# A setup re-planned: second-stage angles on VectorE, four token weight products ahead of the mirrored weights, chunk 0's y evicted sooner

## The chip, the cores and the metric

The kernel runs on one core of one Trainium2 chip. The metric is the device time of one execution in microseconds (us); smaller is better. A time is quoted as the median of several executions with the lowest and highest in brackets. The profile is of one execution, and its span is some 2 us shorter than the time.

Engine names: PE is TensorE, DVE is VectorE, ACT is ScalarE, POOL is GpSimd, SP issues transfers.

## The reference, cut to what matters

```python
def _attn_ref(x):
    X = np.fft.fft(x, axis=1)          # over 3008 tokens
    X = np.fft.fft(X, axis=2)          # over 256 features
    return X.real.astype(np.float32)

def _moe_ref(x, w_tok1, w_tok2, w_ch1, w_ch2):
    xt = x.transpose(0, 2, 1)
    h = np.maximum(xt @ w_tok1, 0.0) @ w_tok2
    u = x + h.transpose(0, 2, 1)
    h2 = np.maximum(u @ w_ch1, 0.0) @ w_ch2
    return (u + h2).astype(np.float32)
# x: 8 x 3008 x 256; w_tok1: 3008 x 256; w_ch1: 256 x 1536
```

The output is the second function of the first. The Fourier transforms are done as matrix products with tables of sines and cosines, which the kernel builds on the chip while the first inputs and weights arrive. That is the setup.

## The kernel before

```python
# Angles of the second-stage table td, made on ACT and reduced on DVE.
for o, n, d, k, off in (...four stretches of md...):
    act(md[:, o:o + n], jrow[:, 0:n], scale=d[:, k:k + 1], ...)
whole(vd[:], md[:])                     # ACT
rest(md[:], vd[:], md[:])               # DVE
...
sin(td[:, 0:65], md[:, 0:65])           # ACT

# POOL: the small table anti, then all weight loads are issued by POOL.
ts(acol[:], pcol[:], -1.0, AT.mult, 127.0, AT.add, eng=G)
ts(anti[:], jrow[:, 0:P], acol[:], AT.is_equal, eng=G)
def load_rest():
    load_wc1(0)                         # wc: channel weights, first half
    ...w2n...
    load_wc1(1)                         # second half
    gdma(wc2[...], ...)                 # second channel weights
# later on POOL, when wc2 has landed: five sums over wc (t1w ... t4w)

# The order of the setup's work.
fold0 = fold(0, V)                      # DVE folds batch 0's input in two halves
filler(12)                              # PE: products whose result nobody reads
take(fold0, 5)                          # first half
ts(ol[:, 0:1], ol[:, 0:1], 2.0, AT.mult)                             # four small
ts(td[:, 0:1], td[:, 64:65], 0.5, AT.mult, ol[:, 0:1], AT.add)       # repairs of
ts(td[:, 65:66], td[:, 64:65], 0.5, AT.mult, ol[:, 0:1], AT.subtract)# td, on DVE
V.memset(td[:, 64:65], 0.0)
take(fold0, 5)                          # second half
own = front(0)                          # stage 1 of batch 0: products pz, results z
take(tu_q, 3); take(tu_p, 2)            # tables tq, tts on PE
take(own, 2)                            # stage 1, first half of the fold
take(tu_r, 3)
filler(4)
take(own, 2)                            # stage 1, second half of the fold
take(tu_b0, 2)
take(own, 4)
...
```

After stage 1 come the second-stage products (pw, from td and z), the token products (ph, from the tables tts and the weights w1p and w1m), and from there chunk after chunk of channel products (pc). Batch 1's input is xp, loaded in rows, and xm, gathered by index. Its fold on DVE (fa, fb, ..., pad) runs in the first chunks of batch 0.

Of the kernel before, what the change touches and what calls it, by code (L numbers as in the profile page):

```python
# [12 lines left out]
AT = mybir.AluOpType  # L13
AFT = mybir.ActivationFunctionType

P = 128
# [3 lines left out]
DTOK = 256  # L20
# [5 lines left out]
NG = 12  # L26
# [10 lines left out]
def kernel(  # L37
# [25 lines left out]
    def ps_mm(name):  # L63
        return psum.tile([P, 512], FP32, tag="mm", name=name, bufs=3)
# [4 lines left out]
    def ps_f(name, dt=FP32, n=512):  # L69
        return psum.tile([P, n], dt, tag="f", name=name, bufs=3)  # L70
# [11 lines left out]
    def ts(out_, in_, s1, op0, s2=None, op1=None, eng=V):  # L82
        if op1 is None:
            eng.tensor_scalar(out=out_, in0=in_, scalar1=s1, scalar2=None, op0=op0)
        else:
            eng.tensor_scalar(out=out_, in0=in_, scalar1=s1, scalar2=s2,
                              op0=op0, op1=op1)
# [7 lines left out]
    def act(out_, in_, scale=1.0, func=AFT.Copy, bias=None):  # L95
        kw = {} if bias is None else {"bias": bias}
        nc.scalar.activation(out=out_, in_=in_, func=func, scale=scale, **kw)  # L97

    def copy(e, out_, in_):
        if e:  # L100
            V.tensor_copy(out=out_, in_=in_)
        else:
            act(out_, in_)
# [111 lines left out]
    def whole(v, m):  # L215
        act(v, m, func=AFT.Identity, bias=tw23[0:m.shape[0], :])

    def rest(r, v, m):
        stt(r, v, -TWO23, m, AT.add, AT.subtract)
# [47 lines left out]
    ts(dr[:], q2[:], 1.0 / 128, AT.mult, 0.0, AT.max)  # L267
    stt(ol[:, 1:2], dl[:, 1:2], 0.5, ol[:, 1:2])
    ts(orr[:], dr[:], 0.5, AT.mult)
    for o, n, d, k, off in ((0, 65, dl, 0, ol[:, 0:1]), (65, 64, dr, 0, None),  # L270
                            (129, 64, dl, 1, ol[:, 1:2]), (193, 64, dr, 1, orr[:, 1:2])):
        if off is None:
            act(md[:, o:o + n], jrow[:, 0:n], scale=d[:, k:k + 1])
        else:
            act(md[:, o:o + n], jrow[:, 0:n], scale=d[:, k:k + 1], func=AFT.Identity, bias=off)
    whole(vd[:], md[:])

    ident, anti, lrot = (const.tile([P, P], FP16, tag=n, name=n)
                         for n in ("ident", "anti", "lrot"))
# [12 lines left out]
    t1b = const.tile([KR, 3, 24], FP16, tag="t1b")  # L292
    t1m = stage.tile([KR, 96], FP16, tag="t1m")
    t1c = stage.tile([KR, 72], FP16, tag="t1c")
    rest(md[:], vd[:], md[:])
    csv = cs[0:KR, 0:4, :].rearrange("p (a b) k -> p a b k", a=2)
    for i in range(2):
# [7 lines left out]
    sin(td[:, 66:258], md[:, 65:257])  # L305


    ts(acol[:], pcol[:], -1.0, AT.mult, 127.0, AT.add, eng=G)
    ts(anti[:], jrow[:, 0:P], acol[:], AT.is_equal, eng=G)
    wc1 = const.tile([P, 2, DCH], FP16, tag="wc1")  # L310
# [120 lines left out]
    def back(k, sgn):  # L431
        for c in range(3):
            c4 = slice(512 * c, 512 * c + 512)
            pr = ps_mm("pr")
            nc.tensor.matmul(pr[:], lhsT=anti[:], rhs=tts[k][:, c4], start=True, stop=True)
            if k:
                act(tts[k + 1][:, c4], pr[:], scale=sgn)
            else:
                V.tensor_copy(out=tts[k + 1][:, c4], in_=pr[:])
            yield  # L440

    hp = const.tile([P, NG, DTOK], FP16, tag="hp")
    hq = const.tile([P, NG, DTOK], FP16, tag="hq")

    def carried():
        for dst, t0, t1 in ((hp, tts[0], tts[1]), (hq, tts[2], tts[3])):
            for g2 in range(NG // 2):
                ph = ps_mm("ph")
                for k in range(2):
                    g = 2 * g2 + k  # L450
                    o = ph[:, k * DTOK:(k + 1) * DTOK]
                    nc.tensor.matmul(o, lhsT=t0[:, g * P:g * P + P], rhs=w1p[:, g, :],
                                     start=True, stop=False)
                    nc.tensor.matmul(o, lhsT=t1[:, g * P:g * P + P],
                                     rhs=w1m[:, NG - 1 - g, :],
                                     start=False, stop=True)
                copy(g2 % 2, dst[:, 2 * g2:2 * g2 + 2, :].rearrange("p g k -> p (g k)"),
                     ph[:])
                yield

# [2 lines left out]
    def front(b):  # L463
# [15 lines left out]
        for t0 in (11, 6, 1):  # L479
            for half in range(2):  # L480
                pz = ps_f("pz")
                for k in range(5):
                    stage1(pz[:, 96 * k:96 * k + 96], eo[:, t0 + k], half, t1r, t1m[:])
                zo = z[:, half, :, :].rearrange("p k (u s) -> p u k s", u=4)
                copy(half == 0 and b > 0, zo[:, :, :, t0:t0 + 5],
                     pz[:, 0:480].rearrange("p (t u k) -> p u k t", t=5, u=4))
                yield
        for half in range(2):
# [44 lines left out]
        def y(c):  # L533
            ps = []
            for o, tab in ((0, tp), (129, tq)):
                py = ps_f("py")
                for k in range(4):
                    nc.tensor.matmul(py[:, P * k:P * k + P], lhsT=w[:, 4 * c + k, o:o + P],  # L538
                                     rhs=tab[:, 4 * c + k, :], start=True, stop=True)
                ps.append(py)  # L540
                if o == 0:
                    yield
            sq = perb.tile([P, CW], FP32, tag="sqy", name="sqy", bufs=2)
            act(sq[:], ps[1][:])
            yield
            pv = ps[0][:].rearrange("p (g i b) -> p g i b", g=4, i=2)
            sv = sq[:].rearrange("p (g i b) -> p g i b", g=4, i=2)
            tt(ytg[:, 0, c], pv, sv, AT.subtract)
            tt(ytg[:, 1, c], pv, sv, AT.add)
            nc.sync.dma_start(out=yrow[c:c + 1], in_=yt[0:1, 1::-1, 8 * c:8 * c + 8, :])  # L550
            yield
# [30 lines left out]
        def tok1():  # L582
            for th in range(2):
                c = slice(th * P, (th + 1) * P)
                pt = ps_f("pt1")
                uv = perb.tile([P, 2, P], FP32, tag="uv", name="uv", bufs=2)
                for o, n, w0, hw in ((0, 129, 0, hp), (129, 127, 130, hq)):
                    if b == 0 and o:
                        sp = perb.tile([P, 129], FP32, tag="sp", name="sp", bufs=1)
                        act(sp[:], pt[:, 0:129])  # L590
                        pt = ps_f("pt2")
                        tt(uv[:, 0, 0:1], sp[:, 0:1], sp[:, P:129], AT.subtract)
                        tt(uv[:, 1, 0:1], sp[:, 0:1], sp[:, P:129], AT.add)
                    for g in range(NG):
                        nc.tensor.matmul(pt[:, o:o + n], lhsT=hw[:, g, c],  # L595
                                         rhs=w[:, g, w0:w0 + n],
                                         start=(g == 0), stop=(g == NG - 1))
                if b == 0:
                    tt(uv[:, 0, 1:], sp[:, 1:P], pt[:, 129:256], AT.subtract)
                    ts(uu[:, th, 0, :], uv[:, 0, :], 0.0, AT.max)  # L600
                    tt(uv[:, 1, 1:], sp[:, 1:P], pt[:, 129:256], AT.add)
                    act(uu[:, th, 1, :], uv[:, 1, :], func=AFT.Relu)
                    yield
                    continue
                sq = perb.tile([P, P], FP32, tag="squ", name="squ", bufs=1)
                act(sq[:], pt[:, P:2 * P])
                tt(uv[:, 0, :], pt[:, 0:P], sq[:], AT.subtract)
                tt(uv[:, 1, :], pt[:, 0:P], sq[:], AT.add)
                ts(uu[:, th, :, :], uv[:], 0.0, AT.max)
                yield  # L610
                if th == 0 and b > 0:
                    yield from rot()

        if b == 0:
            yield from rot()
            yield from y(0)
            yield from tok1()
            y1 = y(1)
            next(y1)
            next(y1)  # L620
            yield
            yield from tok2(0)
            yield from y1
            yield from tok2(1)
            yield from y(2)
            yield from tok2(2)
            for c in (4, 3, 5):
                yield from tok2(c)
        else:
            yield from tok1()  # L630
            for c in range(3):
                yield from y(c)
            for c in (2, 1, 0, 3, 4, 5):
                yield from tok2(c)
# [170 lines left out]
    def take(g, n):  # L805
        for _ in range(n):
            next(g, None)
# [6 lines left out]
    fold0 = fold(0, V)  # L814
    filler(12)
    take(fold0, 5)
    ts(ol[:, 0:1], ol[:, 0:1], 2.0, AT.mult)
    ts(td[:, 0:1], td[:, 64:65], 0.5, AT.mult, ol[:, 0:1], AT.add)
    ts(td[:, 65:66], td[:, 64:65], 0.5, AT.mult, ol[:, 0:1], AT.subtract)
    V.memset(td[:, 64:65], 0.0)  # L820
    take(fold0, 5)
    own = front(0)
    take(tu_q, 3)
    take(tu_p, 2)
    take(own, 2)
    take(tu_r, 3)
    filler(4)
    take(own, 2)
    take(tu_b0, 2)
    take(own, 4)  # L830
# [118 lines left out]
```

## Time and profile before

The kernel before took 601.85 us (601.52 to 602.42, three runs).

| | before |
|---|---|
| span of the profiled execution | 599.8 us |
| PE busy | 582.5 us, 97% |
| first channel product on PE | 33.63 us |
| fold of batch 1 starts on DVE | 42.12 us |
| product on pad starts on PE | 62.34 us |

The prediction below shows the page and the chain of waits.

### The profile page before, as it was taken

The page shows a single profiled execution, that of the slowest core. Times are in us where ns is not written, and L with a number is a line of the kernel's source. Part 1 is how long each engine was busy: PE and PEld are TensorE (multiplying, and loading weights), DVE is VectorE, ACT ScalarE, POOL GpSimd, SP SyncE. Part 2 cuts the span into 40 slices and gives each one's busy share as a digit, 9 for nine tenths or more (in the row PEclk, how much of TensorE's full clock was granted, in tenths as well). Part 3 has the DMA queues.
Part 4 walks back from the last instruction along what each step waited for, and adds up shares of the span by engine and source line. Part 5 has one row for each costly group of instructions (what it writes and reads, how often), then busy time and mean ns, then how long its engine had stood idle before and what let it go on. Part 6 is the DMA issues. An engine that isn't in the chain of part 4 may idle for free.

```text
span 599.8 us, 15331 instructions
## 1 busy us (share of the span) xinstructions
PE 582.5 (97%) x6273; PEld 417.8 (70%) x6273; DVE 449.5 (75%) x924; ACT 390.2 (65%) x753; POOL 255.1 (43%) x396
## 2 busy tenths in 40 slices
PE   3899999999999999999999999999999999999997
PEld 3756676677767776667767777677766777666776
DVE  8769879685898668766898668856688757966663
ACT  8764665478647865477656867568665786556662
POOL 8550545937555554626348444565555000000000
PEclk9999999999999999999999999999999999999999
DMA  8992822277138913394335753376133422323533
GB/s 158 207 192 61 170 50 53 61 149 119 37 71 121 149 37 68 78 181 54 68 84 91 135 89 55 67 147 113 37 60 80 93 55 55 77 61 77 93 72 88
DMA packets 83414, 55.69 MB, mean 93 GB/s; under 512 B 53778, under 2 KB 80082, under 8 KB 82578
## 3 DMA queue, kind: packets, MB, share of 16 engines
q1 hardware_dynamic: 76816, 36.82, 31.9%
q0 software_dynamic: 6208, 17.63, 16.2%
q8 instruction: 49, 0.80, 0.6%
q10 hardware_dynamic: 320, 0.26, 0.2%
q14 instruction: 21, 0.17, 0.1%
HBM read 35.26 MB, written 24.64 MB: 100 GB/s over the span
## 4 chain that ended last, share of the span: by engine, by line
PE 82%; DVE 1%; issue 0%; DVEq 0%
PE pc L662 36%; PE pa L712 17%; PE pb L712 13%; PE pu L566 6%; PE po L775 4%; PE pt L595 3%; PE pz L471 1%; PE py L538 1%; PE pw L512 1%; PE pw L508 1%; DVE s L90 1%; DVE osb L90 0%; DVE ut L90 0%; PE pz L496 0%; DVE q L90 0%
## 5 line engine op out<-in xcount | busy, mean ns | idle before, releaser
L97 ACT ACTIVATE c<-pc 128x512 f16<-128x512 f32 (+1 forms) x553 | 314.4, 591 | 156.2 <-PE pc L662 138.7
L662 PE MATMUL pc<-ut,wc 128*128 128x512 f16 (+1 forms) x1152 | 316.5, 374 | 1.2 <-DVE ut L90 1.2
L712 PEld LDWEIGHTS <-s 128*128 128x128 f16 x1968 | 123.5, 98 | 37.5 <-DVE s L90 0.6
L662 PEld LDWEIGHTS <-wc 128*128 128x128 f16 x1152 | 97.0, 98 | 50.7 <-issue 3.0
L712 PEld LDWEIGHTS <-c 128*128 128x128 f16 x1476 | 93.0, 97 | 27.8
L90 DVE TENSOR_TENSOR q<-pa,uT 128x256 f32<-128x256 f32 x123 | 52.5, 427 | 47.6 <-PE pa L712 47.5
L90 DVE TENSOR_TENSOR s<-c 128x1536 f16<-128x1536 f16 x82 | 80.7, 984 | 4.7 <-ACT c L97 4.7
L908 POOL COPY hold<-s 128x1 f16<-128x1 f16 x29 | 5.4, 187 | 173.5 <-DVE s L90 173.5
L90 DVE TENSOR_TENSOR osb<-pb,q 128x256 f32<-128x256 f32 x123 | 52.0, 422 | 23.8 <-PE pb L712 20.3
L90 DVE TENSOR_TENSOR ut<-pu,yt 128x512 f16<-128x512 f32 (+1 forms) x96 | 63.3, 672 | 0.8 <-PE pu L566 0.4
L90 POOL TENSOR_TENSOR eo<-sab 96x512 f16<-96x512 f16 x48 | 52.7, 1114 | 1.6
L566 PE MATMUL pu<-w2r,uu 128*128 128x512 f16 (+1 forms) x168 | 50.0, 379 | 0.3 <-DVE ut L90 0.3
L90 POOL TENSOR_TENSOR sab<-fa,fb 96x256 f16<-96x256 f16 (+1 forms) x72 | 46.7, 673 | 0.0
L90 DVE TENSOR_TENSOR s<-s,c 128x1536 f16<-128x1536 f16 x41 | 40.4, 986 | 0.0
L97 ACT ACTIVATE w<-pw 128x257 f16<-128x257 f32 x90 | 34.8, 387 | 8.4 <-PE pw L512 5.5
L90 DVE TENSOR_TENSOR s<-c,s 128x1536 f16<-128x1536 f16 x41 | 39.0, 952 | 0.0
L775 PE MATMUL po<-wc,c 128*128 128x256 f16 x288 | 35.4, 273 | 0.0
L712 PE MATMUL pb<-wc,c 128*128 128x128 f16 x492 | 34.4, 219 | 0.0
L712 PE MATMUL pa<-wc,c 128*128 128x128 f16 x492 | 34.4, 219 | 0.0
L712 PE MATMUL pa<-t2w,s 128*128 128x128 f16 x492 | 34.2, 219 | 0.1
L712 PE MATMUL pb<-t1w,s 128*128 128x128 f16 x492 | 34.2, 219 | 0.0
L712 PE MATMUL pa<-t4w,c 128*128 128x128 f16 x492 | 34.2, 219 | 0.0
(187 smaller groups left out, 728.0 us busy)
## 6 DMA issues: line engine op xcount, KB each, us to landing
out_dram<-osb SPq DMA_DIRECT2D x83, 256.0 KB
xp<-in_x_dram POOLq DMA_DIRECT2D x14, 408.0 KB, 6.4
out_dram<-osb SPq DMA_DIRECT2D x11, 192.0 KB
uT<-ut SPq DMA_TRANSPOSE x96
w2n<-in_moe_w_tok_dram POOLq DMA_DIRECT2D x2, 752.0 KB, 9.8
w1p<-in_moe_w_tok_dram POOLq DMA_DIRECT2D x2, 384.0 KB, 8.2
wc<-in_moe_w_ch_dram POOLq DMA_DIRECT2D x1, 768.0 KB, 15.3
xp<-in_x_dram POOLq DMA_DIRECT2D x2, 272.0 KB, 5.7
```

Source lines behind the costliest of these rows:

```text
L90: eng.tensor_tensor(out=out_, in0=a, in1=b, op=op)
L97: nc.scalar.activation(out=out_, in_=in_, func=func, scale=scale, **kw)
L471: nc.tensor.matmul(out_, lhsT=rows[:, half * P:half * P + P], rhs=tab, start=True, stop=True)
L508: nc.tensor.matmul(pw[:, 0:256].rearrange("p (h d) -> p h d", h=2)[:, :, 0:65], lhsT=zg[:, 0, g], rhs=td[:, 0:130].rearrange("p (h d) -> p ...
L512: nc.tensor.matmul(pw[:, 64:322].rearrange("p (h d) -> p h d", h=2)[:, :, 0:64], lhsT=zg[:, 1, g], rhs=td[:, 130:258].rearrange("p (h d) - ...
L538: nc.tensor.matmul(py[:, P * k:P * k + P], lhsT=w[:, 4 * c + k, o:o + P], rhs=tab[:, 4 * c + k, :], start=True, stop=True)
L566: nc.tensor.matmul(pu[:, 0:64 * nk], lhsT=uu[:, th, h, :], rhs=w2[:, th, :, 8 * c:8 * c + nk], start=(th == 0), stop=(th == 1))
L595: nc.tensor.matmul(pt[:, o:o + n], lhsT=hw[:, g, c], rhs=w[:, g, w0:w0 + n], start=(g == 0), stop=(g == NG - 1))
L662: nc.tensor.matmul(pc[:, 0:n], lhsT=wc1[:, h, ct * P:(ct + 1) * P], rhs=ut[:, c, h, 0:n], start=(h == 0), stop=(h == 1))
L712: nc.tensor.matmul(dst[:, P * a:P * a + P], lhsT=left[:, k, a, :], rhs=right[:, k, :], start=(first and k + a == 0), stop=(k == NH - 1), s ...
L775: nc.tensor.matmul(po[:, o:o + D], lhsT=c1[:, ct, ks * P:ks * P + P], rhs=wc2[:, ct, 0:D], start=(ct == 0), stop=(ct == NCT - 1))
L908: G.tensor_copy(out=hold[:], in_=pbox[3][:, 0, 0, 0:1])
```

## The change

The intent is to get PE to its first dense stretch sooner. The angles leave ACT, so that its large sine tp can start earlier. The four repairs of td leave DVE for POOL, between the fold's two halves. Four products on w1p take the place of four fillers ahead of the second half of stage 1 (the change's title says eight; four stand there). Stage-1 results are evicted by two engines, and y of chunk 0 is interleaved differently. Besides, the table products tu_r move ahead of the first half of stage 1, and a few evictions of tts and hq change engines (left out of the cut below).

```diff
-    for o, n, d, k, off in (...):
-        ...act(md[:, o:o + n], jrow[:, 0:n], scale=d[:, k:k + 1], ...)
-    whole(vd[:], md[:])
 ...
+    for o, n, d, k, off in (...):
+        ...ts(md[:, o:o + n], jrow[:, 0:n], d[:, k:k + 1], AT.mult, ...)
+    ts(vd[:], md[:], TWO23, AT.add)
     rest(md[:], vd[:], md[:])
 ...
+    ts(ol[:, 0:1], ol[:, 0:1], 2.0, AT.mult, eng=G)
+    ts(td[:, 0:1], td[:, 64:65], 0.5, AT.mult, ol[:, 0:1], AT.add, eng=G)
+    ts(td[:, 65:66], td[:, 64:65], 0.5, AT.mult, ol[:, 0:1], AT.subtract, eng=G)
+    G.memset(td[:, 64:65], 0.0)
     ts(acol[:], pcol[:], -1.0, AT.mult, 127.0, AT.add, eng=G)
     ts(anti[:], jrow[:, 0:P], acol[:], AT.is_equal, eng=G)
 ...
     def carried():
+        early = [ps_out("ph", k) for k in range(2)]
+        for g in range(4):
+            one(early[g // 2], tts[0], w1p, g, g, g % 2 == 0)
+        yield
 ...  # the other products follow, w1p first and then w1m, pair by pair
-                copy(half == 0 and b > 0, zo[:, :, :, t0:t0 + 5],
+                copy(half == 0 if b else half and t0 < 11, zo[:, :, :, t0:t0 + 5],
 ...
-            yield from y(0)
-            yield from tok1()
+            y0, t1 = y(0), tok1()
+            for piece in (y0, y0, y0, t1, t1):
+                next(piece)
+                yield
 ...
     take(fold0, 5)
-    ts(ol[:, 0:1], ol[:, 0:1], 2.0, AT.mult)
-    ts(td[:, 0:1], td[:, 64:65], 0.5, AT.mult, ol[:, 0:1], AT.add)
-    ts(td[:, 65:66], td[:, 64:65], 0.5, AT.mult, ol[:, 0:1], AT.subtract)
-    V.memset(td[:, 64:65], 0.0)
     take(fold0, 5)
     own = front(0)
     take(tu_q, 3)
     take(tu_p, 2)
+    take(tu_r, 3)
     take(own, 2)
-    take(tu_r, 3)
-    filler(4)
+    take(car, 1)
     take(own, 2)
```

## The prediction

> **What bounds the kernel now.** I read the page's busy shares and its 40 slices first. TensorE (PE) is busy 582.5 of 599.8 us; all its visible slack is in the first slice, 15 us long. So a change of setup can be worth a few us at most, and 2% of the run is 12 us.
>
> ```profile
> span 599.8 us, 15331 instructions
> PE 582.5 (97%) x6273; PEld 417.8 (70%) x6273; DVE 449.5 (75%) x924; ACT 390.2 (65%) x753; POOL 255.1 (43%) x396
> PE   3899999999999999999999999999999999999997
> ```
>
> Second, the timeline of PE (start, duration, engine, line, operation, in square brackets the idle time before it and what ended it). PE starts at 8.06, waits 1.19 us for VectorE's folded input at 16.02 and 0.41 for ScalarE's z at 19.86; then it is nearly dense until the first channel product at 33.63.
>
> ```profile
> 8.06 1.46 PE L399 MATMUL filler<-lrot,ident 128*128 128x128 f16 x12 [8.06 <-DVE ident L84]
> 16.02 0.93 PE L476 MATMUL pz<-t1n,eo 96*128 96x96 f16 x11 [1.19 <-DVE eo L90]
> 19.86 0.23 PE L508 MATMUL pw<-td,z 128*128 128x130 f16 x1 [0.41 <-ACT z L97]
> 20.21 0.27 PE L454 MATMUL ph<-w1m,tts 128*128 128x256 f16 x1
> 33.63 1.46 PE L662 MATMUL pc<-ut,wc 128*128 128x512 f16 x6 [0.32 <-DVE ut L90]
> 53.14 0.38 PE L662 MATMUL pc<-ut,wc 128*128 128x512 f16 x1 [0.90 <-DVE ut L90]
> 62.34 0.20 PE L496 MATMUL pz<-t1n,pad 96*128 96x24 f16 x2 [0.26 <-DVE pad L90]
> ```
>
> Third, what comes after setup, because a gain there counts only if it survives. The timeline of VectorE (DVE) shows a wait of 2.67 us for the second batch's input (the gathered half xm) until 42.12. From there DVE runs without a gap to 64.1; its next large wait for PE is at 67.75. The two PE waits above, at 53.14 and 62.34, are for results of that gapless run: pad is the end of the second batch's fold.
>
> ```profile
> 42.12 0.77 DVE L90 TENSOR_TENSOR fa<-xp,xm 96x508 f16<-96x508 f16 x1 [2.67 <-DMA xm<-in_x_dram,ix]
> 42.81 1.76 DVE L90 TENSOR_TENSOR fb<-xm,xp 96x508 f16<-96x508 f16 x1
> 44.50 0.18 DVE L90 TENSOR_TENSOR sab<-xp,xm 96x8 f16<-96x8 f16 x1
> 61.91 0.48 DVE L90 TENSOR_TENSOR pad<-sab 96x65 f16<-96x65 f16 x4
> 67.75 0.82 DVE L90 TENSOR_TENSOR osb<-po,uT 128x256 f32<-128x256 f32 x3 [1.55 <-PE po L775]
> ```
>
> Fourth, why xm lands only then: the DMA view of 20 to 45 us. In its 40 slices the DMA engines are full until the landing; the load is the tail of one long saturated queue.
>
> ```profile
> DMA  9998999999999999999999999999799999999999
> q0 software_dynamic: 2625, 4.51, 98.9%
> q1 hardware_dynamic: 1644, 0.40, 17.9%
> ```
>
> Fifth, GpSimd (POOL) in the same time: its weight sums start when the last weights land and end at 42.57 + 1.72 = 44.29.
>
> ```profile
> 36.83 0.23 POOL L646 COPY wc<-wc 128x12 f16<-128x12 f16 x1 [5.92 <-DMA wc<-in_moe_w_ch_dram]
> 41.10 1.51 POOL L90 TENSOR_TENSOR t3w<-b,wc 128x768 f16<-128x768 f16 x1
> 42.57 1.72 POOL L90 TENSOR_TENSOR t4w<-wc,t2w 128x768 f16<-128x768 f16 x1
> ```
>
> **What the Trainium skill says.** The page "SBUF — State Buffer", section "Who interferes with whom", calls the shared port pair an exclusive lock between VectorE and GpSimd, and counts a tensor_tensor with two SBUF inputs among what contends with GpSimd's reads. The trace agrees: fb took 1.76 us at 42.81, ending at 44.57, just after POOL's t4w; the same operation takes 0.41 at 47.36, with POOL idle. "DMA: Bandwidth & Descriptors", section "Issuing engines are not separate DMA queues", says that all issuers use the same 16 engines. In this trace q0 (the loads) fell from 0.21 MB in the microsecond from 40 to 0.14 MB in the next, when q1's packets (transposes issued by SP) rose to 239. "TensorE: Matmul & The Clock Gate", Part 1, has PE slow down after idling; here the granted clock is 0.999 on average, and I give the four removed fillers no cost.
>
> **The change, part by part.** The order view of the two programs gives the moves; beyond the chunk products of batch 0 the sequence on every engine is unchanged.
>
> 1. Angles. ScalarE loses four md and one vd activations, which occupy it from 6.57 to 8.35: 1.8 us. Its large sine (tp) then waits for DVE's m, 6.60 + 0.95 = 7.55, and starts 0.8 us earlier. The first product on tp, at 10.08, comes at about 9.3. DVE gains five small operations. A 128x120 tensor_scalar took 0.28 and a 128x128 one 0.28; I allow 4 x 0.16 + 0.35 = 1.0 us for the five. In before, DVE sat idle 0.47 for vd, so the remainder md moves from 8.48 to about 9.0. The small tables follow, ending at 10.3 in place of 9.8; the fold started at 10.13 because xm landed then, so it starts some 0.2 us late.
>
> 2. The td repairs leave DVE: first-half fold to second-half fold was 12.82 to 13.45, of which 0.6 us goes. Second half: 13.45 + 0.2 - 0.6, so about 13.05, 0.4 us earlier; PE's wait for eo ends at about 15.6 in place of 16.02. POOL carries them instead. Its small operations stand about 0.2 to 0.3 apart, so four make 0.9 us, and the loads issued from 15.12 go out at about 16.0. The queue then still has the mirrored weights (w1m), which land at 9.83 + 9.8 = 19.6, so I cost this at zero.
>
> 3. Products ahead. The words say eight; the order view shows four w1p products placed before the second group of stage-1 products, in place of four fillers. At 0.11 us of start-to-start each they take 0.44 us out of the later stretch. They need w1p: two issues at 6.44 and about 7.15, 7.6 to 8.8 us to land, hence 14.8 to 15.9. That lies in the gap, but can give back up to 0.3 us.
>
> 4. z on two engines. ScalarE's z evictions ran 16.95 + 2.85 = 19.80, five in a row at about 0.55 us. Now two of the large ones go to DVE and one tts eviction comes over. With stage 1 0.2 to 0.4 us earlier and a net saving of one eviction, 0.5, pw starts at about 19.1 to 19.2 in place of 19.86: 0.7 us. Then w1m stands in the way: the first such product was at 20.21 and cannot start before 19.6, so at most 0.6 us passes there.
>
> 5. y of chunk 0 and the last hq. The sequence on PE is the same; DVE gives one hq eviction to ScalarE. PE's wait of 0.19 for hq at 29.98 goes.
>
> Sum at the first channel product: 0.55 (w1m floor) + 0.2 (part of the early products that ScalarE's evictions do not hide; it is busy nearly throughout from 20 to 25 us) + 0.19 = about 0.9 us, so 33.63 becomes about 32.7. I hold 0.4 to 1.4 for possible.
>
> What reaches the end: nothing of it, by the third reading. The xm gather lands when the saturated queue is through, whatever PE does. DVE's order is fixed, so its idle time before the fold grows, from 2.67 towards 3.6; the gapless run starts at 42.12 as before; PE waits at 53.14 for 1.8 in place of 0.9; and by 62.34 both kernels are at the same point. Everything after that is the same program. The sum on the path is 0.
>
> **The rivals.**
>
> A. The gain survives, some 0.9 us, giving 600.9. This needs the landing or DVE's run to move too. For it: if xm came half a us earlier, fa and fb might slip between POOL's operations and escape the 1.35 us that fb lost. Against it: bytes and order of the loads are unchanged and the queue was full throughout.
>
> B. A loss, of 0.2 to 0.6 us, giving 602.2. An earlier PE makes the first transposes on q1 earlier, at about 40.4 in place of 41.3. They then share the DMA engines with the end of the xm gather for 0.9 us longer, at about half: 0.45 us later. POOL's t4w then has the lock, and fa waits until 44.3 with fb behind it. Since fb ended at 44.57 anyway, only about 0.25 to 0.4 of this is new. For it: q0 did fall by a third in that microsecond. Against it: PE must really be early.
>
> C. The longer DVE list delays the front. DVE has 1.0 us more before the fold, and if a small operation costs twice my figure the second half of the fold starts late and PE's gain is gone. This hardly touches the time: DVE idles 2.67 us before 42.12 and PE has 0.9 of wait at 53.14, so under 0.9 us of lateness disappears. It would give 601.8.
>
> **Range and chances.** The central case is no change; A at perhaps one in four pulls by 0.2, B at one in four pushes by 0.1, so 601.7. The three runs of before lie between 601.52 and 602.42, half a us either way of the median; with A's end of 600.9 and B's of 602.3, a range of 600.8 to 602.5 should hold it 8 times in 10. Twelve us one way or the other has no mechanism here: 1% each.
>
> **What would show it right or wrong.** In the new profile: tp's sine at about 7.6; z evictions on both engines and pw at about 19.2; PE waiting for no hq; first channel product near 32.7; DVE's idle before the second batch's fold longer than 2.67 and the fold still at 42.1 plus or minus 0.5; the PE wait near 53 about 1.8; pad reached at about 62.3. If the fold starts a us earlier or later, or if fb takes 0.41 there, the prediction's step on the landing is wrong and A or B holds. If PE stalls for w1p before the second stage-1 group, step 3 is wrong. It would be wrong as a whole if the span fell with the fold unmoved, since PE would then be making up the time somewhere after 62 that I take as equal.

## More of the kernel before

POOL's timeline. The columns are start, duration, engine, line, operation with output and input, sizes and count; a bracket, where there is one, gives the idle time just before and what ended it.

```profile
13.03 0.34 POOL L86 TENSOR_SCALAR ixc<-cfeat 128x1 int32<-128x1 f32 x2
...
13.72 1.45 POOL L84 TENSOR_SCALAR anti<-jrow,acol 128x128 f16<-128x128 f32 x1
15.12 1.17 POOL L106 DMA_DIRECT2D wc<-in_moe_w_ch_dram  x2
...
29.81 0.94 POOL L109 DMA_INDIRECT xm<-in_x_dram,ix  x1 [2.60 <-DMA w2n<-in_moe_w_tok_dram]
```

The small index operations take 0.17 us each, and the first channel weights are issued at 15.12. The last gather of batch 1's xm is issued only at 29.81, after a wait that the profile puts down to the landing of w2n. One line of PE is needed for comparison, two products on anti:

```profile
17.17 0.60 PE L435 MATMUL pr<-tts,anti 128*128 128x512 f16 x2
```

The windows view gives, for each stretch of 2 us, the busy time of PE, weight loads, DVE, ACT and POOL, then the clock granted to PE, the DMA share and the GB/s.

```profile
16.00:18.00 2.00, 1.86 (x32) 1.50 (x33) 1.23 (x7) 1.18 (x3) 1.70 (x3) 1.00 1.12 211
18.00:20.00 2.00, 1.49 (x31) 1.08 (x29) 1.61 (x4) 1.80 (x4) 1.74 (x4) 1.00 1.18 205
20.00:22.00 2.00, 2.00 (x22) 1.58 (x22) 1.43 (x4) 1.65 (x5) 1.69 (x3) 1.00 1.14 208
```

The granted clock is 1.00, and the DMA engines move 205 GB/s or more all the time. The DMA view of 16 to 24 us sums up what that is in bytes:

```profile
DMA packets 766, 1.67 MB, mean 209 GB/s; under 512 B 96, under 2 KB 416, under 8 KB 764
```

## The result, and the profile after

The changed kernel took 604.45 us (603.68 to 605.53, six runs), the kernel before 601.8 in the same rounds. The ratio is 1.0039, with a 95% interval of 1.0019 to 1.0059. The change is a small loss, 2 to 3 us, and it lies above the predicted range.

The page of the profiled execution, which took 603.68 us:

```profile
span 601.3 us, 15324 instructions
PEclk9899999999999999999999999999999999999999
```

The row PEclk is the granted clock in tenths in 40 slices of 15 us. The second slice has an 8, where before has nines throughout. PE's timeline:

```profile
16.51 0.61 PE L452 MATMUL ph<-w1p,tts 128*128 128x256 f16 x4 [1.95 <-DMA w1p<-in_moe_w_tok_dram]
...
18.38 1.05 PE L439 MATMUL pr<-tts,anti 128*128 128x512 f16 x2
...
21.73 0.23 PE L521 MATMUL pw<-td,z 128*128 128x130 f16 x1 [0.26 <-ACT z L97]
...
35.87 1.46 PE L677 MATMUL pc<-ut,wc 128*128 128x512 f16 x6 [0.25 <-DMA wc<-in_moe_w_ch_dram]
...
63.72 0.22 PE L509 MATMUL pz<-t1n,pad 96*128 96x24 f16 x2 [0.26 <-DVE pad L90]
```

The early products wait 1.95 us for w1p. The same two products on anti that took 0.60 us in before take 1.05. The first product on td and z comes 1.87 us later than before (19.86), and the first channel product 2.24 us later (33.63). The windows of 16 to 22 us name the reason for the 1.05:

```profile
16.00:18.00 2.00, 1.49 (x20) 1.45 (x21) 0.69 (x6) 0.18 (x1) 1.77 (x5) 0.79 1.12 210
18.00:20.00 2.00, 2.00 (x20) 1.45 (x18) 1.35 (x2) 1.16 (x2) 1.70 (x4) 0.50 1.06 167
20.00:22.00 2.00, 1.70 (x27) 1.25 (x25) 1.09 (x3) 1.26 (x3) 2.00 (x4) 0.86 0.80 99
```

The granted clock is 0.50 through the whole of 18 to 20 us. In windows of 0.2 us it is 0.50 from about 17.2 to 20.6. In the same rows the DMA engines fall from 210 to 167 and 99 GB/s, where before moved 205 and more. POOL's timeline and the DMA view of 16 to 24 us say why:

```profile
13.53 1.24 POOL L86 TENSOR_SCALAR ixc<-cfeat 128x1 int32<-128x1 f32 x2
...
15.06 1.27 POOL L86 TENSOR_SCALAR td<-td,ol 128x1 f16<-128x1 f16 x2
...
17.43 1.17 POOL L106 DMA_DIRECT2D wc<-in_moe_w_ch_dram  x2
...
30.98 0.93 POOL L109 DMA_INDIRECT xm<-in_x_dram,ix  x1 [2.75 <-DMA w2n<-in_moe_w_tok_dram]
...
43.57 1.73 POOL L90 TENSOR_TENSOR t4w<-wc,t2w 128x768 f16<-128x768 f16 x1
```

```profile
DMA packets 726, 1.38 MB, mean 173 GB/s; under 512 B 97, under 2 KB 417, under 8 KB 725
```

Two operations of 128 x 1 elements take 1.27 us, and the two index operations grew from 0.34 to 1.24. The loads are issued 2.31 us later than in before, the queue ran low, and 0.29 MB less was moved, which at before's 209 GB/s is 1.4 us. The last gather of xm goes out 1.17 us later, at 30.98. POOL's last weight sum ends at 45.30 instead of 44.29. The fold of batch 1 on DVE follows:

```profile
43.31 0.58 DVE L90 TENSOR_TENSOR fa<-xp,xm 96x508 f16<-96x508 f16 x1 [1.62 <-DMA xm<-in_x_dram,ix]
43.82 1.76 DVE L90 TENSOR_TENSOR fb<-xm,xp 96x508 f16<-96x508 f16 x1
```

It starts 1.19 us later than before. The late loads and the late fold are tied by that gather: in all 13 profiles the fold starts 11.6 to 12.9 us after the last gather was issued, and it follows that issue more closely than the issue of the first loads.

**One moment decides everything after it.** In every profile, the span less the start of the first product on pad is the same: 599.8 - 62.34 = 537.5 in before, 601.3 - 63.72 = 537.6 after, and 537.4 to 537.6 in all eleven experiments. So the prediction's sentence "everything after that is the same program" held, and what has to be explained is only when that product starts. It starts when the later of two walls is through: DVE's run from the fold to pad, or PE's own work up to there.

### The profile page after: what moved, and what is told of

Same layout as the page of the kernel before. It is cut to its first block, busy times and chain, and to the rows that moved or that the text cites. A ratio compares the mean times of both kernels' runs of the same rounds, so it can differ in the third digit from the quotient of the medians.

```text
span 601.3 us, 15324 instructions
## 1 busy us (share of the span) xinstructions
PE 584.6 (97%) x6269; PEld 419.9 (70%) x6269; DVE 450.9 (75%) x925; ACT 388.5 (65%) x748; POOL 260.3 (43%) x400
## 4 chain that ended last, share of the span: by engine, by line
PE 81%; DVE 1%; issue 0%; DVEq 0%
PE pc L677 35%; PE pa L727 17%; PE pb L727 13%; PE pu L579 6%; PE po L790 4%; PE pt L608 3%; PE py L551 1%; PE pz L484 1%; DVE s L90 1%; PE pw L525 1%; PE pw L521 1%; DVE osb L90 0%; DVE q L90 0%; DVE ut L90 0%; DVE z L101 0%
## 5 line engine op out<-in xcount | busy, mean ns | idle before, releaser
L90 POOL TENSOR_TENSOR sab<-fa,fb 96x256 f16<-96x256 f16 (+1 forms) x72 | 48.3, 695 | 0.0
```

The lines of the kernel that those rows point to most:

```text
L90: eng.tensor_tensor(out=out_, in0=a, in1=b, op=op)
```

## The experiments

The kernels before and after were taken apart along three suspects: the loads issued late (repairs on POOL), the wait for w1p (early products), and the granted clock. Times of before in the three sessions were 602.01 (601.82 to 606.4, 11 runs), 601.62 (601.18 to 602.44, 9) and 602.3 (601.65 to 603.9, 11).

| run | median us | ratio to before, 95% | clock of its runs | first channel product | fold starts | product on pad |
|---|---|---|---|---|---|---|
| before | 601.8 | | profiled one .999 | 33.63 | 42.12 | 62.34 |
| after | 604.45 | 1.0039 (1.0019 to 1.0059) | four .996 to .997, two 1.0 | 35.87 | 43.31 | 63.72 |
| e1 | 604.07 | 1.0027 (1.0001 to 1.0053) | all six .997 | 35.50 | 43.34 | 64.10 |
| e2 | 603.63 | 1.0027 (0.9999 to 1.0055) | four .990 to .997, two 1.0 | 35.84 | 43.39 | 63.69 |
| e3 | 603.86 | 1.0015 (0.9990 to 1.0039) | four .996 to .997, two .999 | 36.03 | 42.05 | 63.88 |
| e4 | 604.14 | 1.0015 (0.9989 to 1.0041) | all .999 to 1.0 | 34.09 | 44.50 | 64.57 |
| e5 | 601.81 | 1.0009 (0.9995 to 1.0023) | .998 to 1.0 | 34.04 | 41.66 | 61.93 |
| e6 | 603.07 | 1.0024 (1.0010 to 1.0038) | .999 to 1.0 | 34.34 | 43.89 | 64.04 |
| e7 | 602.37 | 1.0012 (0.9998 to 1.0026) | .999 to 1.0 | 34.07 | 43.60 | 63.65 |
| e8 | 601.57 | 1.0004 (0.9990 to 1.0017) | .999 to 1.0 | 34.04 | 42.27 | 61.93 |
| e9 | 601.73 | 0.9992 (0.9974 to 1.0010) | five .999 to 1.0, one .997 | 33.20 | 41.84 | 61.53 |
| e10 | 603.77 | 1.0022 (1.0002 to 1.0041) | four .996 to .999, two 1.0 | 33.64 | 42.43 | 62.66 |
| e11 | 601.52 | 0.9985 (0.9970 to 1.0000) | .999 to 1.0 | 33.56 | 42.00 | 61.42 |

The last three columns are from the one profiled execution of each. The intervals of e2, e3, e4, e5, e7, e8 and e9 include 1; the argument rests on the profiles and on the clock of each run.

### e1: the changed kernel with the repairs back on DVE

> The changed kernel with the four td repairs back on VectorE between the two halves of the fold; the early products stay. Theory T (two separate delays, either of which is enough for over 1 us: PE waits for w1p in front of the second stage-1 group, and GpSimd's repairs hold up the weight loads): GpSimd issues the first wc load before 16.2 us in place of 17.43, the second batch's fold starts at 42.0 to 42.6 in place of 43.31, but PE still waits 1.5 to 2 us for w1p and reaches the first channel product at 35.0 to 36.0; time 1 to 2 us above before. Rival R1 (the late loads are the whole cause): time within 0.5 us of before. Rival R2 (PE's wait is the whole cause): same time as the changed kernel, 2 to 3 us above before.

```diff
-    ts(ol..., eng=G); ts(td[:, 0:1]..., eng=G); ts(td[:, 65:66]..., eng=G); G.memset(td[:, 64:65], 0.0)
 ...
     take(fold0, 5)
+    ts(ol...); ts(td[:, 0:1]...); ts(td[:, 65:66]...); V.memset(td[:, 64:65], 0.0)
     take(fold0, 5)
```

It measured 604.07 us, hardly better than after. The loads were issued at 16.33, 1.10 us sooner, and 1.50 MB were moved between 16 and 24 us. But PE waited 0.65 for w1p and then 0.80 for the fold, the clock was halved from 18.4 to 21.8, and all six runs show a mean clock of 0.997. Undoing the repairs alone does not bring the time back.

### e2: the changed kernel without the early products

> The changed kernel without the early products: each w1p product again beside its w1m product, and the four fillers back in their place; the repairs stay on GpSimd. T: no wait for w1p, the first channel product at 32.7 to 33.7, but the loads still go out at about 17.4, the DMA engines run dry near 20 us, the weight sums start at about 37.8 and the second batch's fold at about 43.3; time 0.7 to 1.3 us above before. R1: as the changed kernel, 2 to 3 us above before. R2: within 0.5 us of before.

```diff
-        early = ...; for g in range(4): one(early[g // 2], ...); yield
 ...
-    take(car, 1)
+    filler(4)
```

It measured 603.63 us. PE's second half of stage 1 began at 15.91 after a wait of 1.27 for the fold, so the wait for w1p is indeed gone. Yet the clock was halved for twice as long as in after. Two windows of 0.2 us show where it began and ended (the clock is the third number from the end):

```profile
16.80:17.00 0.20, 0.20 (x9) 0.20 (x6) 0.00 (x0) 0.16 (x1) 0.16 (x1) 0.70 0.99 184
...
23.60:23.80 0.20, 0.20 (x4) 0.16 (x2) 0.00 (x0) 0.20 (x2) 0.20 (x1) 0.73 1.02 211
```

All windows between those two have 0.50. From 16.9 to 23.7 is 6.8 us. In after it lasted 3.4 us (17.2 to 20.6), in e1 3.4 (18.4 to 21.8) and in e3 3.4 (17.9 to 21.3). The lengths are one or two times 3.4 us. This gives a second reading of the mean clocks: 3.4 us at half speed in 601 us lower the mean by 3.4 x 0.5 / 601 = 0.003. So 0.997 is one such stretch, 0.994 two.

### e3: both undone, the rest of the change kept

> The changed kernel with both undone: repairs on VectorE, no early products; the angles on VectorE, the z split and the earlier y stay. T (and the third reading of the prediction: PE's gain in setup is swallowed by the wait for the second batch): first channel product at 32.6 to 33.5, fold at 42.1 plus or minus 0.4, PE's wait for ut near 53 longer than 0.9, time within 0.5 us of before. Rival R3 (a third part, the angles or the z split, costs too): over 0.7 us above before. Rival R4 (the gain survives): 0.6 us or more below before.

The edit is e1's and e2's together. It measured 603.86 us, so its median lies 1.85 us above that of before without either part, although the interval of its ratio includes 1. The profile is the clearest one for PE:

```profile
36.03 1.45 PE L669 MATMUL pc<-ut,wc 128*128 128x512 f16 x6 [0.33 <-DMA wc<-in_moe_w_ch_dram]
```

```profile
42.05 0.42 DVE L90 TENSOR_TENSOR fa<-xp,xm 96x508 f16<-96x508 f16 x1 [0.20 <-DMA xm<-in_x_dram,ix]
```

The fold starts even sooner than in before, but PE is 2.40 us late at its first channel product. DVE then waits 1.86 us for PE's output po at 48.16, and the span is 601.5. Here PE is the wall. The loads have next to no share in it: the profile puts the last 0.33 us down to wc, but ut, which PE also needs, was no earlier (DVE wrote its two parts from 35.28 to 36.57, so the first was done at about 36.0). Nor is all of PE's lateness the clock: the second half of stage 1 began at 17.20 in place of 16.02 (wait of 1.69 for the fold), and 0.76 of these 1.18 us were there at PE's first product (8.82; the reason is told at e8). The other 1.2 us up to the first product on td and z (22.25 in place of 19.86) came while the clock was halved. The two runs with a mean clock of 0.999 had spans of 600.5 and 600.9, the four at 0.996 to 0.997 had 601.5 to 602.0: about 1 us for the clock.

### e4: the kernel before with only the repairs moved to POOL

> The kernel before with one edit: the four td repairs on GpSimd ahead of anti. T: the repairs cost GpSimd about 2 us because VectorE's fold runs beside them; loads at about 17.2 to 17.5 in place of 15.12, weight sums and fold about 1 us later, PE unchanged until 33.6; time 0.7 to 1.3 us above before. Rival (the repairs cost the 0.9 us that the prediction gave them and the queue hides it): loads at about 16, fold at 42.1, time within 0.4 us of before.

```diff
+    ts(ol..., eng=G); ts(td[:, 0:1]..., eng=G); ts(td[:, 65:66]..., eng=G); G.memset(td[:, 64:65], 0.0)
     ts(acol[:], pcol[:], -1.0, AT.mult, 127.0, AT.add, eng=G)
 ...
-    ts(ol...); ts(td[:, 0:1]...); ts(td[:, 65:66]...); V.memset(td[:, 64:65], 0.0)
```

It measured 604.14 us, all of it at full clock. This is e3's counterpart:

```profile
34.09 1.46 PE L666 MATMUL pc<-ut,wc 128*128 128x512 f16 x6 [0.26 <-DVE ut L90]
```

```profile
44.50 0.62 DVE L90 TENSOR_TENSOR fa<-xp,xm 96x508 f16<-96x508 f16 x1 [4.59 <-DMA xm<-in_x_dram,ix]
```

PE is 0.46 late and has to wait for DVE, 1.10 us at 53.59 and 1.40 at 55.38. The fold is 2.38 late, more than the 1 us expected. The loads went out at 16.94 against 15.12 and 1.39 MB moved between 16 and 24 us, as in after. The two repairs on td took 1.27 us at 14.56 and the index operations 1.24 at 13.04, so this is the cost of moving the repairs alone. The move also brought what it was meant to: the second half of stage 1 began at 15.44 in place of 16.02. PE then lost part of that again, in a wait of 0.30 at 17.05 for anti, which POOL makes after the repairs. Two of its six runs had a span of 600.5, only 0.7 above before's, so the loss varies from run to run even with identical instructions.

### e5: the changed kernel, kept warm, with the loads' delay reduced

> The changed kernel without the early products, with the repairs on VectorE after the whole fold (where VectorE idled 1.9 us), and 20 fillers in place of four in front of the second stage-1 group. Theory T2, from the first four runs: the span is fixed by when PE reaches pad (span minus that time was 537.5 to 537.6 in all six profiles), and three things delay it: the granted PE clock falling to half after a gap, PE waiting for w1p, and late weight loads. With no gap PE stays at full clock: PEclk 1.0 in all windows from 16 to 26 us, first channel product at 32.5 to 33.5; loads at 15.4 to 16.3, at least 1.55 MB moved from 16 to 24 us; time within 0.6 us of before. Rival (the clock falls at random times whatever the gaps): clock still 0.994 to 0.997 in most runs and over 1.2 us above before.

```diff
-    ...repairs on POOL, early products...
 ...
     take(fold0, 5)
     take(fold0, 5)
+    ts(ol...); ts(td[:, 0:1]...); ts(td[:, 65:66]...); V.memset(td[:, 64:65], 0.0)
 ...
-    take(car, 1)
+    filler(20)
```

It measured 601.81 us and a ratio of 1.0009: back to before, though the first channel product at 34.04 missed the expected 32.5 to 33.5 (why is told at e8). The clock stayed at 1.00 over the whole setup, the loads went out at 15.90 and 1.69 MB moved between 16 and 24 us. Angles on VectorE, the moved tu_r, shared evictions and y of chunk 0 are all still in it, so with PE's gap filled they cost nothing, and they bring no gain either. They are not harmless without the fillers: e3 has these parts alone, its gap is 1.69 us against 1.19 in before, and four of its six runs lost the clock.

### e6: the changed kernel with 36 fillers ahead of the early products

> The changed kernel with 36 fillers ahead of the early products, so that PE has work while w1p is awaited; nothing else. T2: w1p lands at 16.4 as before and the loads stay late (17.4), but the clock stays at 1.0; the first channel product comes at 34.0 to 35.0 in place of 35.87, and the time stays 0.9 to 1.8 us above before, since the late loads alone give that. Rival (the clock was the whole loss): within 0.5 us of before. Rival (the clock is a symptom): no change from the changed kernel, clock 0.996 to 0.997.

```diff
+    filler(36)
     take(car, 1)
```

It measured 603.07 us, at full clock in every run. This takes the slow clock away and leaves the late loads. PE is back, DVE is not:

```profile
34.34 1.46 PE L677 MATMUL pc<-ut,wc 128*128 128x512 f16 x6 [0.33 <-DVE ut L90]
```

```profile
43.89 0.71 DVE L90 TENSOR_TENSOR fa<-xp,xm 96x508 f16<-96x508 f16 x1 [3.73 <-DMA xm<-in_x_dram,ix]
```

PE's first channel product comes 1.53 us sooner than in after, and PE then waits 1.40 us for DVE at 54.85. Together with e1 and e5 this makes roughly four corners: neither suspect removed (after, 1.0039), the loads partly relieved (e1, 1.0027), the clock kept (e6, 1.0024), both (e5, 1.0009, which also drops the early products). By these ratios each alone leaves most of the loss, which fits two walls side by side of which the later decides; the intervals overlap, so it is the profiles that show it.

### e7: the kernel before with only the early products

> The kernel before with one edit: the four w1p products in place of the four fillers, the later order pairwise as in the change; repairs, angles, z and y as before. T2: PE waits for w1p until 15.9 to 16.5, longer than the fold needs (16.02), by 0 to 0.5 us; loads on time (15.1), fold at 42.1; where the clock holds, time within 0.5 us of before because PE has 0.9 us to give; where it falls, 1 us or more above. Rival (the products cost by themselves): all runs over 1 us above before with the clock at 1.0.

The edit is the `early` block of the change and `take(car, 1)` for `filler(4)`. It measured 602.37 us, ratio 1.0012. PE waited 1.45 us for w1p until 16.50, although the clock stayed up. The loads were issued at 15.41 and 1.61 MB moved between 16 and 24 us, nearly as in before, but the fold still started at 43.60. The last gather of xm was issued at 30.68 in place of 29.81, which is over half of it; why, the theory does not say, and it is left open below.

### e8: e5 with the second channel weights loaded first

> As e5_kept_warm, with the load of wc2 ahead of the second half of wc1. The third reading says that VectorE's run from the second batch's fold sets the end, and that fb in it waits for GpSimd's weight sums, which start when wc2 lands. wc1's second half is 0.39 MB, about 2 us of queue at 200 GB/s: wc2 lands at about 35, the sums end at about 42.4, fb is over by about 43.3 in place of 44.57, and PE, early by up to 0.9 and with 0.9 of wait to lose, can follow: 0.6 to 1.3 us below before. Rival A: PE reaches the seventh channel product (about 37) before wc1's second half has landed and waits: no gain or a loss. Rival B (the sums are not what holds the fold): same time as e5_kept_warm.

```diff
+        ...wc2 load...
         load_wc1(1)
-        ...wc2 load...
```

It measured 601.57 us, 1.0004. POOL's weight sums ended at 40.27 + 1.54 = 41.81, ahead of the fold, and fb took 0.41 us in place of 1.76. The span was 599.4, against e5's 599.3: no gain. DVE now waited 1.01 us for PE's po at 46.17. The wall had moved to PE.

PE was late in e5 and e8 for a reason that lies much earlier. At 1.87 us DVE computes ix, a tensor_scalar of 128 x 16 elements. In before, after, e2, e4, e6, e10 and e11 it took about 0.95 us and ended some 0.1 us after POOL's iota kb had begun (2.70); in e1, e3, e5, e7 and e8 it took 1.72 and ended when kb ended (3.55). From there on everything on DVE and PE came 0.7 us later: ident at 8.47 instead of 7.72, PE's first product at 8.81 instead of 8.06.

### e9: e8 with POOL's large iota behind the two small ones

> As e8_warm_wc2_first, with GpSimd's longest iota (kb, 0.86 us) issued after krow and jrow in place of before them. In the five edited kernels that had PE's first product at 8.81 in place of 8.06 to 8.10, VectorE's ix took 1.72 us at 1.87 and ended as kb ended (3.55); where it took 0.94 it got in just ahead of kb. If ix waits for whatever GpSimd began first, it now waits for krow at worst, 0.3 us: ix ends by 3.1, PE starts at 8.1 to 8.4, the first channel product comes at 33.2 to 33.7 in place of 34.04. e8's VectorE waited 1.01 us for PE at 46.17, so this gain should reach the end: span 0.3 to 0.8 us below e8, time 0.4 to 1.0 below before. Rival (the race is only a symptom of code placement): PE still starts at 8.8 and time equals e8.

```diff
-    iota(kb[:]..., [[8, 3], [1, 4], [47, 64]], 0, 0)
     iota(krow[:]..., [[8, 3], [1, 4], [4, 2]], 0, 0)
     iota(jrow[:], [[1, 129]], 0, 0)
+    iota(kb[:]..., [[8, 3], [1, 4], [47, 64]], 0, 0)
```

It measured 601.73 us, 0.9992 of before. The operation ix took 0.40 us, PE began at 7.63 and its first channel product came at 33.20, the earliest of all. So the late start of e8 went with the iota, as supposed. But 0.43 us gained on PE against before brought the span only to 599.1: DVE waited 2.82 us for xm until 41.84, 0.59 for po at 45.33 and 0.39 for the transfer uT at 46.14. One of its six runs had the slow clock (0.997) and a span of 601.3.

### e10: the kernel before without its four fillers

> The kernel before without the four fillers ahead of the second stage-1 group: PE's gap there grows from 1.19 to about 1.57 us, nothing else moves. If a gap of that size is what lets the granted clock fall (it held in before with 1.19 and fell in e2_no_early with 1.27), the clock of this kernel falls to about half for some 3.4 us in at least half of the runs, each of those 0.8 us or more above before, and PE's first channel product is late by 1 us or more in such a profile. Rival (what matters is only when in the run the gap comes, or something that the change added): clock stays 0.999 to 1.000 and the time within 0.4 us of before.

```diff
-    filler(4)
```

It measured 603.77 us, ratio 1.0022. Two runs had a clock of 1.0 and spans of 600.2 and 600.3. Two had 0.996 and spans of 602.7 and 603.0: by the sum at e2 that is one lost stretch each. The last two, 0.998 and 0.999 with 602.0 and 601.5, prove no loss: the profiled run of e5 has 0.998 with no halved stretch but the one that begins 1.9 us before the program's end. So two of six runs certainly lost the clock, fewer than the half that was expected. Nothing else in the program is different. In before's eleven runs of the same session the lowest clock was 0.998 and the longest span 601.9; in an earlier session one run of before, too, had 0.996 and 604.4. Two of six against one of 31 suggests that the fillers make the loss rarer, and does not prove it. The profiled execution happened to be one of the undisturbed two, so this run shows the effect in its times and clocks, not in its profile. In it PE waited only 0.78 for the fold and not the expected 1.57, since its products ran at the slow rate until 14.3 and so filled the gap themselves. POOL's loads went out at 15.86 there and at 15.84 in e11, against 15.12 in before, with nothing changed on POOL: so much they vary by themselves.

### e11: the kernel before with the second channel weights loaded first

> The kernel before with one edit: the load of wc2 ahead of the second half of wc1. If VectorE's run from the second batch's fold sets the end in before, and its fb waits for GpSimd's weight sums: wc2 at about 35, sums over by about 42.4, fb takes 0.41 us, the run is about 1.2 us earlier; PE has 0.9 us of wait at 53.14 to lose, so 0.6 to 0.9 us below before. Rival: PE waits for wc1's second half near 37, or the landing of xm moves: no gain.

The edit is e8's, on the kernel before. It measured 601.52 us, 0.9985 of before (0.9970 to 1.0000), so it is the best version. It beats the changed kernel clearly and the kernel before at the edge of what can be told:

```profile
42.00 0.42 DVE L90 TENSOR_TENSOR fa<-xp,xm 96x508 f16<-96x508 f16 x1 [2.61 <-DMA xm<-in_x_dram,ix]
42.34 0.41 DVE L90 TENSOR_TENSOR fb<-xm,xp 96x508 f16<-96x508 f16 x1
```

The weight sums are over at 39.86 + 1.54 = 41.40 and no longer meet the fold. So fb is through 1.8 us sooner than in before (42.75 against 44.57). Half of it survives: DVE next waits 0.80 us for po at 45.70, and the product on pad starts at 61.42 in place of 62.34, a gain of 0.9 us, which the span shows as 599.0 against 599.8.

## Why the prediction was wrong, point by point

**The frame was right.** What follows the product on pad is one and the same program in all profiles (537.4 to 537.6 us), and a gain of PE in the front does not pass the landing of xm: e9 gained 0.43 us at the first channel product and the time moved by a tenth of a per cent. The prediction's "sum on the path is 0" would have been right if its inputs had been.

**Step 1, angles, held in kind.** The sine tp starts at 7.62 (predicted about 7.6) and its first product at 9.37 (about 9.3). The five operations on DVE occupied 7.96 to 9.38, so 1.4 us where 1.0 was allowed, and the first fold starts at 10.61 in place of about 10.3. This is rival C: the second half of the fold began at 13.44, as in before (13.45), so the 0.4 us that step 2 promised there was gone. e5, which contains it, shows that it costs nothing measurable once PE's gap is filled.

**Step 2, the repairs on POOL, failed, and is one of the two causes of the loss.** It allowed 0.9 us for the four operations and then said "I cost this at zero", because the queue would still hold the mirrored weights. The loads went out 2.31 us later, not 0.9. The four repairs took 1.83 us (14.74 to 16.57), the two on td alone 1.27. The prediction had no term for the rest: POOL reached the index operations 0.50 later (13.53 in place of 13.03; not so in e4), these took 0.81 more from start to next start, since DVE's fold now runs beside them, and anti, which now falls behind the fold, gave 0.83 back (0.63 in place of 1.45 us long). Part of the 2.31 can be chance, as e10's 15.86 shows. The Trainium skill's page "SBUF — State Buffer", section "Who interferes with whom", was cited in the prediction for fb alone; the same exclusive lock, for a DVE operation with two SBUF inputs against a POOL operation that reads SBUF, fits these small operations beside the fold (the index operations went from 0.17 to 0.62 us each, the repairs on td took 0.63 each) and the shorter anti behind it. That it is the lock and not another effect no run here isolates. Nor did the queue hide the delay: 1.38 MB instead of 1.67 were moved between 16 and 24 us, and e4 has the same 1.39 from this step alone. The fold came 1.19 us later, which the prediction had named as the sign that its step on the landing was wrong. That step had the xm gather land "when the saturated queue is through"; it left out that POOL issues the last gather only after a wait, by the profile for w2n. In the four runs that moved 1.38 to 1.41 MB between 16 and 24 us (after, e2, e4, e6) this gather went out at 30.98 to 32.55, in the eight that moved 1.57 MB or more at 29.81 to 30.68.

**Step 3, the early products, was under-sized.** It named the wait for w1p, and its landing at 14.8 to 15.9. The weights landed at 16.51, 9.3 us after the issue at 7.19, beyond the 7.6 to 8.8 that before had shown. The second half of stage 1 began at 16.96 in place of 16.02: 0.94 us lost, where 0.3 was allowed. The landing is not steady: the early products could start at 15.82 in e1, 16.50 in e7 and 17.08 in e6.

**Step 4, pw at 19.1 to 19.2, failed by the clock.** Both engines evicted z as foreseen. The product came at 21.73. Of the 1.87 us against before, 0.94 is the late start of stage 1 and the other 0.93 came while PE ran at 0.50. The remaining 0.37 of the 2.24 us at the first channel product came later in small pieces, among them a wait of 0.34 for uu at 34.66.

**The sentence that failed most is "I give the four removed fillers no cost".** It looked at the mean granted clock of 0.999 and not at how close the setup was to losing it. What failed is larger than these four fillers, since e2 and e3 have them back and lost the clock too: it is the zero cost of a gap on PE ahead of the second half of stage 1. e6 shows it best: fillers in that gap, and nothing else, kept the clock in all five runs and brought the first channel product 1.53 us forward. e10 points the same way, with two of six runs at 0.996 and 2.4 to 2.8 us more span than the undisturbed two. The Trainium skill's page "TensorE: Matmul & The Clock Gate", Part 1, says that a free-running window of 3413 ns decides between half and full clock; the traces agree. The transitions that each trace file records (the views print only means, and 1.00 before the first transition) begin with the full rate, at 12.02 in before and 13.74 in after, and in all 13 profiles every later change lies a whole number of 3.41 us after it. The prediction cited that same part, but read only the rule that idling slows PE down. A gap need not be as long as the window: it is enough that it takes up much of one. An estimate from these profiles, waits of PE inside one window: before a drop, 1.95 us in after (57%), 1.69 in e3 (50%), 0.65 + 0.80 in e1 (43%), 1.27 in e2 (37%). With no drop, 1.14 in e11 (33%), 1.01 in e7 (30%), 0.92 in e1's window before (27%), 0.60 in before (18%). In before a window ended at 15.43 and cut the wait of 1.19 in two, in e7 one ended at 16.06 and cut its 1.45. Where the window's edge falls is luck: this is one profile of each kernel.

**Step 5 held.** PE's wait of 0.19 for hq is gone.

**The rivals.** B, a loss of 0.2 to 0.6, had the right sign by the wrong road: it needed an early PE, and PE was late. A did not occur. The actual outcome, late loads and a halved clock, was in no rival.

**How the two losses combine.** They are not added. In after the fold is 1.19 late, and DVE meets PE's po with 0.28 us of waiting at 48.00, so pad is 1.40 late: both walls had moved by nearly the same. e3 shows PE's wall alone (span 601.5), e4 and e6 the loads' wall alone (602.2 and 601.5). Two of after's own runs kept a clock of 1.0 and still had spans of 602.1 and 601.7; they have no trace, but their times suggest that the loss does not need the clock, although single runs of before, too, reached 601.9 at full clock. A reader who removes one cause and sees little improvement (e1, e2, e6) must not conclude that it was none.

**What stays open.**
- What sets the start of the fold to within a us. The bytes moved between 16 and 24 us do not order it (e7 with 1.61 MB starts at 43.60, e3 with 1.60 at 42.05; e4 with 1.39 at 44.50, after with 1.38 at 43.31). The issue of the last xm gather does better: 30.44 in e3, 30.68 in e7, 30.98 in after, 31.69 in e1, 32.55 in e4, each 11.6 to 12.9 us before the fold. Why that issue differs so, with the first loads at 16.94 in e4 and 17.43 in after, no run here shows. A single profile varies here by a us or more.
- Why two of e4's six runs had a span of 600.5 and four 602.1 to 602.6.
- What sets the phase of the clock's window, and why e2's second stretch of 3.4 us stayed slow although PE was busy. For e7 the cut at 16.06 explains why the profiled run kept its clock with a gap of 1.45 us; its other four runs kept it too, and have no trace.

## What to carry to other kernels

Before moving small operations to an idle engine, ask what that engine does next: here it was the issuer of the loads, and some 1.8 us of small operations emptied a queue that looked full. Fillers in a wait are not waste to be cleaned up; count PE's idle time against a window of 3.4 us, and look at the clock in windows of a fraction of a us, since the mean of the whole run hides a stretch that costs a us. When several changes make no difference one by one, look for two walls side by side, find the moment that both release, and measure everything at that moment.

## What the Trainium skill lacked or had wrong

- "TensorE: Matmul & The Clock Gate", Part 1, puts the half clock after at least one idle window of about 3.4 us. Here PE fell to 0.50 with idle gaps of 1.27 to 1.95 us in an otherwise busy stretch. Part 1 also tells of a kernel whose short idles made the clock oscillate, but states no figure for how much idle time in one window is enough; by the estimate above it lies between 33% (e11, no drop) and 37% (e2, drop).
- "SBUF — State Buffer" gives no length for small operations on POOL that may meet the lock: operations of 128 x 1 took about 0.63 us each beside the fold, where the index operations had taken 0.17.
- "DMA: Bandwidth & Descriptors", section "Issuing engines are not separate DMA queues", calls the time that an issue takes on its sequencer usually small relative to the transfer. It does not speak of an issuer that is held up by its own work: here an issue 2.31 us later let the shared queue run down by 0.29 MB, and the last gather of that queue was issued 1.17 us and landed 1.2 us later.
